# Gate and up matmuls as full-row matmuls with grouped remainders, or all as pairs of 64-row tiles

## The chip, the core and the metric

The kernel runs on one core of a Trainium2 chip. Its engines are named as in the profile: PE (TensorE: matmuls, and PEld its weight loads), DVE (VectorE), ACT (ScalarE), POOL (GpSimd) and SP (SyncE, which here only issues DMAs). The metric is the device time of one execution in microseconds (us). Times below are us unless another unit is given.

## The reference, cut to what matters

The sequence has 2048 rows, D = 576 columns, F = 4608 hidden columns; all tensors are bfloat16.

```python
kv = conv4(k, shift_k) * v                       # four taps along the rows
y = irfft(rfft(pad(kv)) * rfft(pad(ssm_k)))[:S]  # a long causal convolution
x = x + ga * (ln(x) * (1 + ca) + sa) * (y + kv * ssm_D)
h = ln(x) * (1 + cb) + sb
out = x + gb * ((silu(h @ w1) * (h @ w3)) @ w2)  # w1, w3: 576 x 4608, w2: 4608 x 576
```

ga, ca and the others are columns of silu(c) @ w_mod. The matmuls with w1 (the gate) and w3 (up) contract over 576 = 4 x 128 + 64 rows.

## The kernel before, in words

The 2048 rows go in four row blocks of 512 (each of two blocks of 256). For each row block `stream` computes h3 = silu(gate) * up, 36 items of 128 hidden columns by 512 rows, and `down` multiplies h3 with w2. Beside `stream` and `down` of row block r runs the convolution of the two blocks of row block r + 1, as a generator (`conv`, and `conv_second` for block 1) that `advance` steps forward: each step yields its cost, each item of `stream` adds to what is due. The convolution is done blockwise with Fourier matrices: `x_spectrum` and `w_spectrum` transform with matmuls (`forward` for blocks 0 and 1, `forward2` later), `pair` multiplies and adds spectra on DVE (operations of 128x3456), `inverse` transforms back with matmuls.

An item fills one PSUM tile `ps` of two banks, gate in the one and up in the other. The PSUM pool has four such tiles, which the items and the convolution's matmuls share. Of the five row tiles that are contracted, four have 128 rows and one has 64. `full` (line 916) does the eight matmuls with 128 rows; `rest` (line 927) does the two with 64 rows, gate from partitions 0 to 63 and up from 64 to 127, which PE runs side by side in the two halves of its array. Items are taken in groups of `size`, two, or four in the last row block, so that the remainders of the group stand together: early items full then rest, late items rest then full. `hide` then empties the tile with two ACT operations (sg, line 934, silu; u, line 936, a copy), DVE multiplies them into h3 (line 938), and `advance` lets the convolution go on.

A first pass, before row block 0's own stream, does rows 0 to 255 of the first 24 hidden chunks (six jobs of four chunks, where an item holds two chunks by 256 rows), while the convolution of block 1 is still under way. Row block 0 then does rows 256 to 511 of these chunks, in jobs of two items, alternating with jobs of four items that do whole chunks.

The weights come in jobs of four chunks (`load_w13`): four DMAs on SP, two of 512 KB (line 871) and two of 64 KB (line 872). There are two buffers `wst`; the last nine chunks of the tile h3 are a third one for the first six loads (FIRST_USE), when nothing of h3 stands there yet. The last three chunks of the first pass keep their weights for row block 0.

Layer norms: ACT sums rows and squares (`ln_sums`, tile junk, line 442, four operations for a block), POOL works out the scales in six small operations (`ln_scales`, lines 457 to 462), and ACT applies them (hg, line 502, and h2row, line 568). POOL's queue has little else.

Each engine takes its instructions in program order. SP's queue issues DMAs in order too, each after its own waits. PE's order is that in which the functions are called.

The lines that the change and the prediction's steps touch are these:

Of the kernel before, what the change touches and what calls it, by code (L numbers as in the profile page):

```python
# [27 lines left out]
FIRST_USE = (0, 1, 2, 0, 1, 2)  # L28
# [16 lines left out]
class _Kernel:  # L45
    def __init__(self, ctx, tc, q, k, v, shift_k, ssm_k, ssm_D, w1, w3, w2, c, w_mod, out):
        self.tc, self.nc = tc, tc.nc
        self.q, self.k, self.v = q, k, v
        self.shift_k, self.ssm_k, self.ssm_D = shift_k, ssm_k, ssm_D
        self.w1, self.w3, self.w2, self.c, self.w_mod, self.out = w1, w3, w2, c, w_mod, out  # L50
        pool = lambda name, **kw: ctx.enter_context(tc.tile_pool(name=name, **kw))
        self.const = pool("const", bufs=1)
        self.psum = pool("psum", bufs=4, space=bass.MemoryType.PSUM)
        self.dram = pool("spill", bufs=1, space=bass.MemoryType.DRAM)
        self.spec = pool("spec", bufs=4)
        self.wprev = pool("wprev", bufs=2)
        self.prod = pool("prod", bufs=1)
        self.acc = pool("acc", bufs=1)
        self.ld = pool("ld", bufs=1)
        self.kvp = pool("kvp", bufs=1)  # L60
        self.x1p = pool("x1p", bufs=4)
        self.lnp = pool("lnp", bufs=1)
        self.small = pool("small", bufs=4)
        self.hp = pool("hp", bufs=2)
        self.w2p = pool("w2p", bufs=NW2)
        self.xo, self.hg, self.accs, self.l1 = {}, {}, {}, {}
        self.X, self.V, self.Wl = {}, {}, {}
        self.n_w13, self.w13, self.kept = 0, {}, {}

# [4 lines left out]
    def setup(self):  # L74
        nc, const = self.nc, self.const
        nc.scalar.preload_act_table(ACT.Silu)
        self.ident = const.tile([P, P], BF16, name="ident")
        self.npi = const.tile([P, 1], F32, name="npi")
# [8 lines left out]
        self.wst.append(self.h3[:, NF - 9:NF, :])  # L87
# [205 lines left out]
    def forward(self, basis, rhs, dst):  # L293

        nc = self.nc
        for e in range(2):
            for cs in range(2):
                ps = self.ps()
                for cc in range(2):
                    for h in range(2):  # L300
                        nc.tensor.matmul(ps[:, h, 0:H], basis[:, cc * (e + 1), cs],
                                         rhs[:, cc, h * H:(h + 1) * H],
                                         start=(cc == 0), stop=(cc == 1))
                nc.scalar.copy(dst(e, cs).rearrange("p (h d) -> p h d", h=2), ps[:, :, 0:H])  # L304
                yield 0.4

    def forward2(self, basis, rhs, both, odd, diff):
# [3 lines left out]
        for cc, dst in ((0, both), (1, odd)):  # L311
            for cs in range(2):
                ps = self.ps()
                for h in range(2):
                    nc.tensor.matmul(ps[:, h, 0:H], basis[:, cc, cs], rhs[:, cc, h * H:(h + 1) * H],  # L315
                                     start=True, stop=True)
                nc.scalar.copy(dst[:, cs].rearrange("p (h d) -> p h d", h=2), ps[:, :, 0:H])  # L317
                yield -1.9
# [39 lines left out]
    def k_rows(self, s):  # L358
# [5 lines left out]
        for cc in range(2):  # L364
            for ct in range(5):
                nc.tensor.transpose(pt[:, cc, ct * P:(ct + 1) * P], nat[:, ct, cc:B:2],
                                    self.ident[:])
        nc.scalar.copy(kT[:], pt[:, :, 0:D])
# [162 lines left out]
    def inverse(self, s, cc):  # L531
        nc = self.nc
        z = self.accs[s]
        ps = self.ps()
# [4 lines left out]
        for i, (b, cs, row) in enumerate(terms):  # L539
            for h in range(2):  # L540
                nc.tensor.matmul(ps[:, h, 0:H], self.Fb[:, b, cs], z[:, row, h * H:(h + 1) * H],  # L541
                                 start=(i == 0), stop=(i == len(terms) - 1))
        return ps
# [27 lines left out]
    def turn(self, pt, cc):  # L571
        for ct in range(5):
            self.nc.tensor.transpose(pt[:, cc, ct * P:(ct + 1) * P],  # L573
                                     self.h2row[:, cc, ct * P:(ct + 1) * P], self.ident[:])
# [20 lines left out]
    def turned(self, s, pt, c0, n):  # L595
# [4 lines left out]
        for ct in range(5):  # L600
            dst = hT[:, ct, t * P:(t + n) * P].rearrange("p (c t) -> p c t", c=n)
            src = pt[:, c0:c0 + n, ct * P:(ct + 1) * P]
# [27 lines left out]
    def first_block(self):  # L630
# [62 lines left out]
        ps = [self.inverse(0, cc) for cc in range(2)]  # L693
# [39 lines left out]
    def outcome(self, s, fill, waits, between=None, quick=False):  # L733


        def steps():
# [4 lines left out]
            for cc in range(2):  # L741
                nc.scalar.copy(y[:, cc, :].rearrange("p (h d) -> p h d", h=2), self.inverse(s, cc)[:, :, 0:H])  # L742
# [118 lines left out]
    def load_w13(self, fc):  # L861
        nc = self.nc
        if self.n_w13 < len(FIRST_USE):
            t = self.wst[FIRST_USE[self.n_w13]]
        else:
            t = self.wst[self.n_w13 % NW13]
# [7 lines left out]
    def advance(self, cost):  # L874

        self.due += cost
        while self.due > 0 and self.steps is not None:
# [5 lines left out]
            self.spent += c  # L883

    def stream(self, r, jobs, rate, size):
# [11 lines left out]
        gus, ws = {}, {}  # L897
# [12 lines left out]
        def full(k, first):  # L910
            (fc, t0, t1, _, _), fi, m = items[k]
            w, n = ws[fc, t0, t1], t1 - t0
            for a in range(m):
                for i in range(2):
                    for ct in range(4):
                        nc.tensor.matmul(gus[k][:, i, a * n:(a + 1) * n],  # L916
                                         w[:, 5 * i + ct, (fi + a) * P:(fi + a + 1) * P], hT[:, ct, t0:t1],
                                         start=(first and ct == 0 and a == 0),
                                         stop=(not first and ct == 3 and a == m - 1))

        def rest(k, first):
            (fc, t0, t1, _, _), fi, m = items[k]
            w, n = ws[fc, t0, t1], t1 - t0
            for a in range(m):
                for i in range(2):
                    rows = slice(64 * i, 64 * i + 64)
                    nc.tensor.matmul(gus[k][:, i, a * n:(a + 1) * n],  # L927
                                     w[rows, 4, (fi + a) * P:(fi + a + 1) * P], hT[rows, 4, t0:t1],
                                     start=(first and a == 0), stop=(not first and a == m - 1))

        def hide(k):
# [9 lines left out]
            self.advance(rate * 2.05)  # L941
# [5 lines left out]
        for k in range(0, len(items), size):  # L947
            early, late = range(k, k + size // 2), range(k + size // 2, k + size)
            for m in early:
                begin(m)  # L950
                full(m, True)
            for m in early:
                rest(m, False)
            for m in late:
                begin(m)
                rest(m, True)
            for m in early:
                hide(m)
            for m in late:
                full(m, False)  # L960
                hide(m)
# [47 lines left out]
    def end(self):  # L1009
        self.advance(1e9)  # L1010

    def run(self):
# [5 lines left out]
        with self.tc.issue_after(last):  # L1018
            self.begin(self.conv_second())
            self.stream(0, [(fc, 0, 256, None, None) for fc in range(n1)], RATE1, 2)  # L1020
# [6 lines left out]
    def row_blocks(self, n1):  # L1027
        for r in range(NRB):
# [8 lines left out]
            if r == 0:  # L1037

                jobs = [(fc, 256, 512, self.kept[fc], None) for fc in (n1 - 3, n1 - 2, n1 - 1)]
# [3 lines left out]
                again = [(fc, 256, 512, None, None) for fc in range(n1 - 3)]  # L1043
# [5 lines left out]
            self.stream(r, jobs, rate, 4 if r == NRB - 1 else 2)  # L1049
# [55 lines left out]
```

## Time and profile before

| | us |
|---|---|
| median of three runs | 523.05 (522.37 to 525.87) |
| the profiled execution | 522.37 |
| its span | 520.6 |
| PE busy | 496.6 |
| DVE busy | 341.1 |
| ACT busy | 293.3 |
| POOL busy | 55.0 |
| idle of PE before gate/up matmuls of 128 rows, 128x512 | 3.5 |

| stage | stretch of the span | length |
|---|---|---|
| opening: block 0's convolution | 0 to 33.7 | 33.7 |
| first pass | 33.7 to 70 | 36.3 |
| row block 0: stream, down | 70 to 137, 137 to 172 | 67, 35 |
| row block 1: stream, down | 172 to 250, 250 to 293 | 78, 43 |
| row block 2: stream, down | 293 to 372.6, 372.6 to 409 | 79.6, 36.4 |
| row block 3: stream, down | 409 to 481, 481 to 520.6 | 72, 39.6 |

How to read the lines of a profile: a line of the order of time has its start, its length, the engine, the line of the kernel, the operation, output<-inputs with shapes, and how many equal ones are merged; in brackets the idle time before it and what ended it. The ends of matmuls are modelled and overlap the next one's start, so the distance of starts is what counts. In the table of the costliest groups a line has the busy time, the mean length in ns, and the engine's idle time before it by what ended it.

### The profile page before, as it was taken

What the parts mean: (1) busy time and instruction counts of PE and PEld (TensorE: products, weight loads), DVE (VectorE), ACT (ScalarE), POOL (GpSimd) and SP (SyncE); (2) the same over time, 40 slices, a digit from 0 to 9 for tenths busy, and PEclk for the clock granted to TensorE, in tenths of its full rate; (3) what the DMA queues carried; (4) which work ended last, traced back from release to release, by engine and by line L of the source; (5) the groups of instructions that cost most, each with busy time, mean ns of one, the idle gap of its engine ahead of it and who ended that gap; (6) DMA issues with size and microseconds to landing.
All of it is one profiled execution on the core that took longest, in us unless ns stands there. A gap on an engine that the chain in (4) does not pass through costs nothing.

```text
span 520.6 us, 8705 instructions
## 1 busy us (share of the span) xinstructions
PE 496.6 (95%) x3351; PEld 292.1 (56%) x3351; DVE 341.1 (66%) x515; ACT 293.3 (56%) x581; POOL 55.0 (11%) x109
## 2 busy tenths in 40 slices
PE   6988989999999999999997999999999999999996
PEld 3656766555687544344785643434588544444775
DVE  8799997999994355897999995389661212212012
ACT  5748679678543469759551465876816446446000
POOL 3403001304030001202001000120101000000000
PEclk9989999999999999999999999999999999999999
DMA  8996909566679953648999884454455553450462
GB/s 280 331 288 196 271 27 351 186 196 203 181 236 313 336 170 115 204 143 291 360 366 313 324 273 159 157 185 152 154 142 144 147 173 124 156 174 3 122 176 68
DMA packets 100989, 106.59 MB, mean 205 GB/s; under 512 B 5011, under 2 KB 93012, under 8 KB 100948
## 3 DMA queue, kind: packets, MB, share of 16 engines
q1 hardware_dynamic: 100926, 106.04, 63.8%
q8 instruction: 26, 0.43, 0.3%
q14 instruction: 15, 0.12, 0.1%
q10 hardware_dynamic: 22, 0.01, 0.0%
HBM read 94.82 MB, written 11.21 MB: 204 GB/s over the span
## 4 chain that ended last, share of the span: by engine, by line
PE 72%; DVE 13%; ACT 7%; DMA 5%; issue 2%; POOL 1%; SPq 0%; POOLq 0%; DVEq 0%; ACTq 0%
PE ps L916 38%; PE ps L979 23%; PE ps L927 6%; DMA w2t<-in_B_w_dram 3%; DVE p L412 2%; PE ps L315 2%; ACT junk L442 1%; DVE h L938 1%; DVE z L407 1%; DVE kv L337 1%; PE ps L541 1%; DVE z L414 1%; DMA wst<-in_B_w_dram 1%; DMA knat<-in_A_ssm_k_dram 1%; ACT X L304 1%
## 5 line engine op out<-in xcount | busy, mean ns | idle before, releaser
L916 PE MATMUL ps<-h2T,wst 128*128 128x512 bf16 (+1 forms) x1248 | 255.1, 356 | 3.5 <-ACT h2T L603 1.6
L916 PEld LDWEIGHTS <-wst 128*128 128x128 bf16 x1248 | 118.7, 98 | 124.0 <-issue 20.0
L934 ACT ACTIVATE sg<-ps 128x512 bf16<-128x512 f32 x144 | 87.0, 604 | 115.6 <-PE ps L927 69.7
L979 PE MATMUL ps<-w2t,h 128*128 128x288 bf16 x1152 | 145.8, 286 | 5.8 <-DMA w2t<-in_B_w_dram 3.9
L979 PEld LDWEIGHTS <-h 128*128 128x128 bf16 x1152 | 112.2, 98 | 35.6 <-issue 6.5
L938 DVE TENSOR_TENSOR h<-sg,u 128x512 bf16<-128x512 bf16 x144 | 60.4, 422 | 95.7 <-ACT u L936 95.7
L936 ACT CAST u<-ps 128x512 bf16<-128x512 f32 x144 | 84.8, 589 | 0.4 <-DVE h L938 0.4
L412 DVE TENSOR_TENSOR p<-X,V 128x3456 bf16<-128x3456 bf16 x28 | 54.7, 1952 | 7.6 <-DMA X<-Xd 6.0
L414 DVE TENSOR_TENSOR z<-z,p 128x3456 bf16<-128x3456 bf16 x28 | 54.7, 1952 | 0.2
L997 DVE TENSOR_TENSOR og<-ps,gbrow 128x288 bf16<-128x288 f32 x32 | 13.2, 450 | 48.8 <-PE ps L979 48.8
L927 PE MATMUL ps<-h2T,wst 64*128 64x512 bf16 (+1 forms) x312 | 40.8, 357 | 0.0
L442 ACT ACTIVATE junk<-x 128x576 bf16<-128x576 bf16 x54 | 37.7, 699 | 0.5
L603 ACT ACTIVATE h2T<-ps,sbcol,cbcol 128x256 bf16<-128x256 bf16 x35 | 16.7, 569 | 26.8 <-PE ps L573 26.8
L927 PEld LDWEIGHTS <-wst 64*128 64x128 bf16 x312 | 10.3, 94 | 26.6 <-issue 23.9
L457 POOL TENSOR_SCALAR l2m<-l2s 128x2 f32<-128x2 f32 x6 | 8.2, 1366 | 153.3 <-ACT junk L442 153.3
L336 DVE TENSOR_TENSOR kvt<-kh,shk 128x1152 bf16<-128x1152 bf16 x24 | 18.1, 753 | 6.7 <-DMA kh<-in_A_k_dram 6.6
L457 POOL TENSOR_SCALAR l1m<-l1s 128x2 f32<-128x2 f32 x7 | 5.9, 847 | 142.1 <-ACT junk L442 142.1
L568 ACT ACTIVATE h2row<-x,l2n,l2r 128x576 bf16<-128x576 bf16 (+1 forms) x24 | 13.8, 652 | 11.6 <-POOL l2n L462 11.6
L337 DVE TENSOR_TENSOR kv<-kv,kvt 128x1152 bf16<-128x1152 bf16 x24 | 18.1, 753 | 0.3
L317 ACT CAST X<-ps 128x576 bf16<-128x576 f32 x24 | 15.7, 664 | 0.0
L407 DVE TENSOR_TENSOR z<-X,V 128x3456 bf16<-128x3456 bf16 x7 | 13.7, 1952 | 1.8 <-DMA X<-Xd 1.8
L742 ACT CAST y<-ps 128x576 bf16<-128x576 f32 x14 | 8.4, 650 | 10.7 <-PE ps L541 10.6
(140 smaller groups left out, 377.5 us busy)
## 6 DMA issues: line engine op xcount, KB each, us to landing
wst<-in_B_w_dram SPq DMA_DIRECT2D x74, 512.0 KB, 4.6
w2t<-in_B_w_dram SPq DMA_DIRECT2D x72, 288.0 KB, 3.5
X<-Xd SPq DMA_DIRECT2D x8, 864.0 KB, 5.6
Xd<-X SPq DMA_DIRECT2D x6, 864.0 KB, 8.1
kh<-in_A_k_dram SPq DMA_DIRECT2D x7, 720.0 KB, 7.4
wst<-in_B_w_dram SPq DMA_DIRECT2D x74, 64.0 KB, 2.2
Vd<-V SPq DMA_DIRECT2D x4, 864.0 KB, 6.1
V<-Vd SPq DMA_DIRECT2D x4, 864.0 KB, 6.4
```

What stands on the lines that cost most here:

```text
L336: nc.vector.tensor_mul(tmp[:], kh[:, 3 - j:5 - j, :], tap(j))
L337: nc.vector.tensor_add(kv[:], kv[:], tmp[:])
L407: nc.vector.tensor_mul(self.accs[s][:], X[:], V[:])
L412: nc.vector.tensor_mul(p[:], X[:], V[:])
L414: nc.vector.tensor_add(z[:], z[:], p[:])
L442: self.nc.scalar.activation(junk[:], src[:, i, :], func, accum_out=out[:, col:col + 1])
L916: nc.tensor.matmul(gus[k][:, i, a * n:(a + 1) * n], w[:, 5 * i + ct, (fi + a) * P:(fi + a + 1) * P], hT[:, ct, t0:t1], start=(first and ct ...
L927: nc.tensor.matmul(gus[k][:, i, a * n:(a + 1) * n], w[rows, 4, (fi + a) * P:(fi + a + 1) * P], hT[rows, 4, t0:t1], start=(first and a == 0 ...
L934: nc.scalar.activation(sg[:], gus[k][:, 0, :], ACT.Silu)
L936: nc.scalar.copy(u[:], gus[k][:, 1, :])
L938: nc.vector.tensor_mul(self.h3[:, f:f + m, t0:t1], sg[:].rearrange("p (a t) -> p a t", a=m), u[:].rearrange("p (a t) -> p a t", a=m))
L979: nc.tensor.matmul(acc[t], self.h3[:, f0 + f, t * P:(t + 1) * P], w[:, f, :], start=(f0 + f == 0), stop=(f0 + f == NF - 1))
```

## The change

All gate and up matmuls, and the convolution's matmuls and transposes that are called while a stream is running (`self.halves`), are done with 64 rows: what was one matmul over 128 rows is two over 64, one for each half of the partitions. At any time one half of the array works on gate and the other on up (for the convolution: on the left and on the right 288 columns), so the two write different banks of the tile; then they swap. Between the two parts each bank passes from one half of the array to the other. For that a token is used: a memset of one element on POOL waits for the last matmul of the first part, and the first matmul of the second part waits for the memset. The items are staggered: the first part of item k+1 is issued before the second part of item k, and for the convolution `advance` breaks off after a first part, so that a part of the stream stands between. An item's first part has ten half matmuls (five pairs), its second eight. The buffer in h3 is no longer used: `wst` has two buffers, the first pass keeps two jobs' weights for row block 0 in place of three, and one job more is read again. Groups of two or four items are gone.

```diff
+    def token(self):
+        first = self.newest()
+        self.nc.gpsimd.memset(self.tok[:], 0.0)
+        self.wait_for(self.newest(), first)
+        return self.newest()
+
+    def two_banks(self, outs, terms):
+        mm = self.nc.tensor.matmul
+        if not self.halves:
+            for n, term in enumerate(terms):
+                for i in range(2):
+                    mm(outs[i], *term(i, slice(0, P)), start=(n == 0), stop=(n == len(terms) - 1))
+            return
+        for swap in range(2):
+            for n, term in enumerate(terms):
+                for rows, i in ((slice(0, 64), swap), (slice(64, P), 1 - swap)):
+                    mm(outs[i], *term(i, rows), start=(swap == 0 and n == 0),
+                       stop=(swap == 1 and n == len(terms) - 1))
+                    if swap == 1 and n == 0 and i == 1:
+                        self.wait_for(self.newest(), mark)
+            if swap == 0:
+                mark = self.token()
+                self.pause = True
+                yield 0.0
...
-        self.wst.append(self.h3[:, NF - 9:NF, :])
...
     def advance(self, cost):
...
             self.spent += c
+            if self.pause:
+                self.pause = False
+                break
...
-        def full(k, first):
+        def part(k, swap):
             (fc, t0, t1, _, _), fi, m = items[k]
             w, n = ws[fc, t0, t1], t1 - t0
             for a in range(m):
-                for i in range(2):
-                    for ct in range(4):
+                cols = slice((fi + a) * P, (fi + a + 1) * P)
+                for ct in range(4 if swap else 5):
+                    for rows, i in ((slice(0, 64), swap), (slice(64, P), 1 - swap)):
                         nc.tensor.matmul(gus[k][:, i, a * n:(a + 1) * n],
-                                         w[:, 5 * i + ct, (fi + a) * P:(fi + a + 1) * P], hT[:, ct, t0:t1],
-                                         start=(first and ct == 0 and a == 0),
-                                         stop=(not first and ct == 3 and a == m - 1))
+                                         w[rows, 5 * i + ct if ct < 4 else 4, cols], hT[rows, ct, t0:t1],
+                                         start=swap == 0 and ct == 0 and a == 0,
+                                         stop=swap == 1 and ct == 3 and a == m - 1)
+                        if swap == 1 and ct == 0 and a == 0 and i == 1:
+                            self.wait_for(self.newest(), marks[k])
+            if swap == 0:
+                marks[k] = self.token()
...
-        for k in range(0, len(items), size):
-            early, late = range(k, k + size // 2), range(k + size // 2, k + size)
-            for m in early:
-                begin(m)
-                full(m, True)
-            for m in early:
-                rest(m, False)
-            for m in late:
-                begin(m)
-                rest(m, True)
-            for m in early:
-                hide(m)
-            for m in late:
-                full(m, False)
-                hide(m)
+        self.halves = True
+        for k in range(len(items) + 1):
+            if k < len(items):
+                begin(k)
+                part(k, 0)
+                self.advance(rate * 2.05 * 5 / 9)
+            if k > 0:
+                part(k - 1, 1)
+                hide(k - 1)
+                self.advance(rate * 2.05 * 4 / 9)
+        self.halves = False
...
-                jobs = [(fc, 256, 512, self.kept[fc], None) for fc in (n1 - 3, n1 - 2, n1 - 1)]
+                jobs = [(fc, 256, 512, self.kept[fc], None) for fc in (n1 - 2, n1 - 1)]
...
-                again = [(fc, 256, 512, None, None) for fc in range(n1 - 3)]
+                again = [(fc, 256, 512, None, None) for fc in range(n1 - 2)]
```

In the changed program PE has 4881 matmuls in place of 3351, and POOL 196 tokens, 144 for the items and 52 for the convolution. Where a stream is running, a block's ten transposes of 128x128 become 18 or 20 of 64x64, and the copy of kT is two ACT operations.

## The prediction

> **What bounds the kernel now.** I read the page's busy line first, then a table by stage, then the instructions in order of time inside one stage, then the waits and the DMA issues.
>
> ```profile
> PE 496.6 (95%) x3351; PEld 292.1 (56%) x3351; DVE 341.1 (66%) x515; ACT 293.3 (56%) x581; POOL 55.0 (11%) x109
> PEclk9989999999999999999999999999999999999999
> ```
>
> TensorE (PE) is busy nearly throughout, at the full granted clock. The table by stage (columns: stretch, length, PE, weight loads, DVE, ACT, POOL, clock, DMA share, GB/s) shows the first pass (24 half chunks), then the gate/up streams of row blocks 0, 1, 2 and 3; the down projections lie between them.
>
> ```profile
> 33.70:70.00 36.30, 34.33 (x310) 26.31 (x310) 33.24 (x55) 24.31 (x47) 5.59 (x8) 0.96 0.69 202
> 70.00:137.00 67.00, 61.65 (x457) 38.02 (x455) 62.96 (x82) 51.25 (x104) 12.29 (x18) 1.00 0.65 213
> 172.00:250.00 78.00, 78.00 (x403) 32.32 (x401) 54.74 (x82) 57.51 (x116) 7.75 (x18) 1.00 0.63 210
> 293.00:372.60 79.60, 79.19 (x411) 33.12 (x409) 58.49 (x83) 55.35 (x111) 5.16 (x14) 1.00 0.55 179
> 409.00:481.00 72.00, 72.00 (x363) 30.34 (x362) 16.47 (x41) 36.74 (x71) 0.00 (x0) 1.00 0.40 130
> ```
>
> DVE is nearly full in the first two rows (33.2 of 36.3, 63.0 of 67.0), where PE has little slack too; in the last three PE alone sets the time. What the change attacks is visible in PE's order of time in row block 1:
>
> ```profile
> 202.35 1.89 PE L916 MATMUL ps<-h2T,wst 128*128 128x512 bf16 x8
> 204.18 0.61 PE L927 MATMUL ps<-h2T,wst 64*128 64x512 bf16 x4
> 204.71 0.42 PE L315 MATMUL ps<-kv,Fb 128*128 128x288 bf16 x2
> ```
>
> In the last stage 16 full matmuls follow each other in 3.45 us, 0.216 each. Here eight take 204.18-202.35 = 1.83, 0.10 more than 8 x 0.216; the two pairs of half-row matmuls take 0.53, again 0.10 more than 2 x 0.216. So a pair costs one full matmul, and each change between full rows and half rows costs 0.10. Weight loads also show it: idle 0.42 before each change.
>
> Three more views carry the costs: ACT's bursts beside PE, Pool's chain, and the weight loads.
>
> ```profile
> 238.50 1.63 ACT L502 ACTIVATE hg<-x,l1n,l1r 128x576 bf16<-128x576 bf16 x2
> 239.41 0.60 PE L927 MATMUL ps<-h2T,wst 64*128 64x512 bf16 x4
> ...
> 240.20 3.62 PE L916 MATMUL ps<-h2T,wst 128*128 128x512 bf16 x16
> ...
> 241.89 0.59 ACT L934 ACTIVATE sg<-ps 128x512 bf16<-128x512 f32 x1
> 243.03 0.59 ACT L936 CAST u<-ps 128x512 bf16<-128x512 f32 x1
> 243.50 0.70 ACT L442 ACTIVATE junk<-x 128x576 bf16<-128x576 bf16 x1
> 244.28 3.63 PE L916 MATMUL ps<-h2T,wst 128*128 128x512 bf16 x16
> ```
>
> ACT works without a gap from 238.0 to 247 here, hg, layer-norm sums (junk), X, sg and u in turn, and PE runs on: four PSUM tiles were enough.
>
> ```profile
> 0.24 0.10 POOL L1089 MEMSET const-float32-0.0<- 128x1 f32 x1 [0.24 <-issue]
> 199.20 0.19 POOL L458 TENSOR_SCALAR l1v<-l1q 128x2 f32<-128x2 f32 x1
> 200.54 0.20 POOL L462 TENSOR_TENSOR l1n<-l1m,l1r 128x2 f32<-128x2 f32 x1
> ```
> ```profile
> wst<-in_B_w_dram SPq DMA_DIRECT2D x74, 512.0 KB, 4.6
> ```
>
> A memset takes 0.10; a layer norm's chain on Pool takes 1.5 from l1v to l1n, and the waits put 299 us of Pool's idle time down to ACT's sums. A 512 KB weight transfer lands 4.6 after its issue.
>
> **The change part by part.** *Switches removed.* The 144 gate/up items stand now in 54 groups of two and 9 of four, each with two switches: 126 x 0.10 = 12.6 us, by stage 1.2, 2.4, 3.6, 3.6, 1.8. Afterwards nine pairs an item (18 half matmuls) take the nine slots of today. Left are about eight switches at the down projections and gate piece: +0.8. The convolution's matmuls are 288 wide; 512- and 256-wide pairs both cost what full ones cost (0.216, 0.109), so theirs cost nothing extra. The transposes become up to 20 of 64x64; bounds are half and equal the 0.66 that ten take today, which is small either way.
>
> *Tokens.* An item's first part (5 pairs, 1.08) is followed by the other item's second part (4 pairs, 0.86) and the next item's first part before its own second part: 1.9 us for PE's end (0.17 after the last start), the memset (0.10, up to 0.20 for other tiny operations) and two semaphores. Hidden. A convolution token has one stream part, 0.86 or more: hidden also, against about 0.5. What ends the cover is Pool's queue: a token issued behind a layer-norm chain waits for ACT's sums and then 1.5 us. Row block 1's first chain, by the changed order: two drains of 0.47 and four sums of 0.77 after PE's part, chain 1.5, token: 6.0; PE arrives at 5.0. It waits 1.0.
>
> *PSUM tiles held longer.* An item is now open for two first and two second parts, 3.9 us, where an early item is open for 2.3; a convolution tile is open for a stream part more. Two items, the convolution's tile and the one being drained fill all four, and in the order the next item's first matmul waits for the copy of the convolution tile just finished. PE's cover for it is 0.86+0.12, the copy needs 0.17+0.66+0.05: 0.1 us left. So each burst on ACT in a convolution phase now stalls PE: the two hg operations (1.6) cost 1.1; the sums of the second l1, worked through in order, 2.2; hg and the l2 sums together 3.7 (sg 3.8 after the convolution's first matmul, u's end 5.6, PE ready at 2.2). In the profile such stalls are nil (PE idles 0.4 in all of row block 1). Row block 1: 1.0+1.1+2.2+3.7 = 8.0 less 3.6, +4.4. Row block 2 has the same bursts, the last one at the end of its stream (2.2): 6.6-3.6 = +3.0. Bounds each: -3.6, if a burst on ACT stays free as above, and +8. I take the worked orders, since the rows for ACT are these very operations.
>
> The Trainium skill's page "TensorEngine Tiling (Array Packing)", in Restrictions and Gotchas, speaks against the change here: it warns that row tiling increases PSUM pressure, different row tiles needing different banks. Today's rows show none of it, with 0.4 of idle; by today's row these two stages would gain 7.2, by the page they would lose part or all of it.
>
> *Weight buffers.* In the staggered order a chunk's buffer is free only after the next job's first part. Today's reload has the whole next job as cover. Both 512 KB transfers are now issued together at the end: 0.2+4.6+0.5 for the second = 5.3 us. With four-item jobs the cover is three items, 5.8: just hidden. In row block 0 two-item jobs alternate with four-item ones and leave one item, 1.95 (with convolution matmuls 2.45 and 3.0). Four loads wait: 2.85+3.35+2.3+3.35 = 11.9. Queued behind the waiting matmul are the stream and the convolution's matmuls, so ACT and DVE starve with them. Bursts on ACT there cost about 5 more; 2.4 of switches go; of today's 6.8 us of PE stalls some 4 go, as DVE gets ahead. +10.5. Bounds: -2.4, if DVE covers all, and +16. On SP the waiting loads also stand ahead of k, x and Xd transfers, which are early enough. One more chunk is read (1.18 MB), beside a DMA that is 0.65 busy: nothing.
>
> *First pass.* The third buffer goes, so four loads have one-item covers; the first wait falls beside PE's wait for kv, which ended at 45.4. The x spectrum's sixteen matmuls, 2.1 in one piece at 45.4, are now spread over two items, +3.9, and DVE's sums wait for them at 48.4 on the chain that ended last. Less 1.2: +2.7; bounds -1.2 and +6.
>
> *Row block 3* has no convolution: -1.8; at worst 0.3 a load, +0.6. The down projections keep full rows: 0.
>
> Sum: 2.7+10.5+4.4+3.0-1.8+0.8 = +19.6 on the profiled execution's 522.4 (span 520.6 and 1.8 around it) is 542.0. Runs of before have the median 523.05, 0.7 above it; within the error I forecast 542.
>
> **The rivals.** *Only the buffers cost.* PSUM and ACT behave as in the profile, so row blocks 1 and 2 keep -3.6 each, and row block 0 pays 11.9-2.4-4 = +5.5. 2.7+5.5-3.6-3.6-1.8+0.8 = 0: 522. For it speaks that nine us of ACT without a gap were free; against it that all four tiles are now held.
>
> *Faster.* PE's switches are the bound everywhere and every wait lies beneath work that DVE or PE has anyway: -12.6+0.8 = -11.8, 511. For it: PE's 95%. Its place is row block 0, where DVE's 63 of 67 would have to cover the loads; it decides while all waits together stay below 11.8, against some 31 by the sums above.
>
> *Pool is slower than assumed.* Operations on Pool took up to 0.68 in place of 0.20 beside a DVE operation, and the longest, beside five of them, 3.2. If a memset is held like that, by one DVE operation of 1.95, the 52 convolution tokens lose about 0.6 each: +31, some 570. Against it: the memset rows of 0.10. The Trainium skill's page "SBUF — State Buffer", Who interferes with whom, says that two-input Vector operations hold up only Pool operations that read SBUF; by it the memsets go free, by the row they don't, and no memset in the trace lies beside such an operation.
>
> **How the numbers follow.** Forecast 0.58, buffers only 0.16, faster 0.14, Pool slower 0.12. Changes of 1%, 5 us, are about what a measurement of this kernel can tell from none. Faster holds the 0.14. Within 1%: 0.14, most of the second case and a little of the first. Slower: 0.72, the rest. The range leaves out the faster case and the upper part of the Pool case: 521 to 565. The forecast's own range is 528 to 558, by the bounds of row block 0 (-2.4 to +16) and the two next (each up to 4 either way), which will not all fall on one side.
>
> **What would show it.** Right: no idle between half-row matmuls of different lines, nine pairs in 1.94; PE waits for wst by DMA, near 3 us, four times in row block 0; PE waits for ACT (X, u) in row blocks 1 and 2, and for Pool's token behind l1n and l2n; row block 3 near 70. Wrong: row blocks 1 and 2 at 74 to 76 (then PSUM was not short); row block 0 at 67 or below (then DVE covered the loads); token memsets lasting over 0.5, or waits for them away from the layer norms (then Pool is the cost).

## The result and the profile after

The changed kernel takes 601.3 us (median of four runs, 600.6 to 602.8) beside 522.7 for the kernel before on the same chip: a ratio of 1.150, 95% interval 1.144 to 1.156. The profiled execution took 601.6, its span is 599.5. I had forecast 542 with a range of 521 to 565: slower was right, the size was not.

TensorE's busy line and its granted clock, in 40 slices, of the kernel after:

```profile
PE 513.7 (86%) x4881; PEld 325.0 (54%) x4881; DVE 345.9 (58%) x515; ACT 298.1 (50%) x586; POOL 65.6 (11%) x305
PEclk9887878898889999999979999998899999999999
```

Busy time grew by 17 us only; the rest of the 79 is time in which TensorE did nothing. And the clock line, nines with a single eight before, has sevens and eights nearly all through the first pass and row block 0 and a few more in row blocks 1 and 2, the stages in which a convolution runs beside the matmuls. The table by stage of the kernel after (stretch, length, PE, weight loads, DVE, ACT, POOL, clock, DMA share, GB/s):

```profile
32.70:70.00 37.30, 25.14 (x340) 19.62 (x340) 20.59 (x28) 17.17 (x34) 9.44 (x19) 0.82 0.47 147
70.00:178.50 108.50, 79.58 (x971) 53.91 (x968) 81.21 (x112) 57.09 (x114) 12.83 (x67) 0.87 0.47 152
218.00:313.30 95.30, 80.51 (x730) 42.31 (x730) 59.01 (x84) 58.96 (x116) 13.05 (x68) 0.95 0.53 179
357.90:452.00 94.10, 79.89 (x731) 40.60 (x730) 56.42 (x80) 57.33 (x114) 9.95 (x68) 0.96 0.45 143
489.80:560.00 70.20, 69.93 (x649) 31.35 (x648) 15.99 (x40) 36.99 (x70) 3.21 (x36) 1.00 0.42 134
```

The first two rows are the first pass and row block 0 (together 96.3 us before, from the start of the first to the start of the last stream matmul; 145.9 now), then row blocks 1, 2 and 3 (78.0 to 95.2, 78.1 to 94.1, 71.6 to 70.2). Only the last one, which has no convolution, gained. In the stages where DVE was nearly full it now works 21 us of 37 and 81 of 108, so the amount of its work isn't the bound.

What TensorE waited for, in all stages (us in total, times, longest):

```profile
PE ps L974 <- DMA wst<-in_B_w_dram: 19.0, 10, 3.2
PE ps L974 <- POOL tok L83: 12.8, 4, 7.1
PE ps L98 <- POOL tok L83: 12.2, 9, 4.0
PE ps L98 <- ACT u L988: 11.0, 7, 3.3
PE ps L974 <- ACT u L988: 10.2, 13, 2.7
...
PE ps L974 <- ACT X L352: 3.4, 3, 1.6
```

Three sorts of waits, each of 19 to 25 us: weights (19.0), tokens (25.0), PSUM tiles that ScalarE had not read yet (24.6). In the kernel before no such line, for a stream's or the convolution's matmuls, is above 1. The fourth part of the loss is no wait. Three stretches of the table by stage inside row block 1:

```profile
278.20:281.10 2.90, 0.25 (x4) 0.00 (x0) 2.90 (x3) 1.03 (x2) 0.00 (x0) 1.00 0.60 209
281.20:282.20 1.00, 1.00 (x10) 0.56 (x11) 1.00 (x3) 0.00 (x0) 0.00 (x0) 1.00 0.00 0
282.30:285.60 3.30, 3.30 (x20) 1.44 (x18) 1.33 (x4) 3.01 (x6) 0.09 (x1) 0.52 0.00 0
```

TensorE waits for most of 2.9 us, runs ten half matmuls in 1.0, and then for 3.3 us has a granted clock of 0.52, where 20 half matmuls are started in place of some 31. PE shows as busy all through these 3.3 us: only the clock column tells. In the trace the half clock comes in stretches of 3.41 us or a multiple; there are 61.4 us of it in the span, 3.4 before.

Count each matmul at the distance of starts that its width has at full clock, a pair of halves as one full matmul, and put down the same time nearly once more to the clock where it starts at half clock. The four gate/up stages then divide so: the matmuls themselves 299.2 (300.1 before), lost to half clock 24.5 (1.4), switches between full and half rows 0.2 (12.4), waits and small gaps, which is the rest, 81.4 (10.1). That is -0.9+23.1-12.2+71.3 = +81.3, as the stage lengths give; the opening and the down projections are 0.8 and 1.5 shorter. The switches went as forecast. The waits and the clock ate more than seven times as much.

### The profile page after: what moved, and what is told of

It is laid out like the page before. It is cut to its first block, busy times and chain, and to the rows that moved or that the text cites. A ratio compares the mean times of both kernels' runs of the same rounds, so it can differ in the third digit from the quotient of the medians.

```text
span 599.5 us, 12152 instructions
## 1 busy us (share of the span) xinstructions
PE 513.7 (86%) x4881; PEld 325.0 (54%) x4881; DVE 345.9 (58%) x515; ACT 298.1 (50%) x586; POOL 65.6 (11%) x305
## 4 chain that ended last, share of the span: by engine, by line
PE 54%; DMA 13%; DVE 13%; ACT 11%; POOL 4%; issue 3%; SPq 1%; ACTq 0%; POOLq 0%
PE ps L974 29%; PE ps L1026 20%; DMA wst<-in_B_w_dram 7%; DMA w2t<-in_B_w_dram 4%; ACT junk L488 4%; DVE z L460 4%; DVE p L458 3%; ACT u L988 2%; ACT sg L986 2%; DMA h<-in_w_mod_dram 2%; POOL l1m L503 2%; PE ps L98 1%; PE ps L93 1%; ACT hg L548 1%; DVE h L990 1%
## 5 line engine op out<-in xcount | busy, mean ns | idle before, releaser
L974 PE MATMUL ps<-h2T,wst 64*128 64x512 bf16 (+1 forms) x3024 | 324.7, 364 | 46.9 <-DMA wst<-in_B_w_dram 19.0
L974 PEld LDWEIGHTS <-wst 64*128 64x128 bf16 x3024 | 170.4, 99 | 178.3 <-issue 30.3
L83 POOL MEMSET tok<- 1x1 f32 x196 | 17.5, 89 | 366.0 <-PE ps L974 305.6
L98 PE MATMUL ps<-kv,Fb 64*128 64x288 bf16 x128 | 18.8, 306 | 14.4 <-POOL tok L83 7.9
L98 PEld LDWEIGHTS <-Fb 64*128 64x128 bf16 x208 | 14.2, 105 | 30.3 <-issue 13.3
L799 ACT CAST y<-ps 128x576 bf16<-128x576 f32 x14 | 8.8, 647 | 18.4 <-PE ps L93 12.7
L98 PE MATMUL ps<-kT,Fk 64*128 64x288 bf16 x64 | 10.1, 296 | 5.7 <-POOL tok L83 4.3
```

What stands on the lines that cost most here:

```text
L83: self.nc.gpsimd.memset(self.tok[:], 0.0)
L98: mm(outs[i], *term(i, rows), start=(swap == 0 and n == 0), stop=(swap == 1 and n == len(terms) - 1))
L974: nc.tensor.matmul(gus[k][:, i, a * n:(a + 1) * n], w[rows, 5 * i + ct if ct < 4 else 4, cols], hT[rows, ct, t0:t1], start=swap == 0 and c ...
```

## The experiments

**Theory.** Three separate sorts of wait, not one bound, and on top of each the half clock that follows a long idle time of TensorE. **Rivals:** one bound behind all waits (VectorE), so that taking one away only uncovers the next; the halved convolution as such; the weight buffers as such.

**Tokens behind a layer norm.** The longest wait, in the first pass of the kernel after (timeline):

```profile
35.68 6.40 POOL L503 TENSOR_SCALAR l1m<-l1s 128x2 f32<-128x2 f32 x1 [1.11 <-ACT junk L488]
...
44.29 0.23 POOL L83 MEMSET tok<- 1x1 f32 x2
44.43 3.81 PE L974 MATMUL ps<-h2T,wst 64*128 64x256 bf16 x34 [7.07 <-POOL tok L83]
```

The two tokens take 0.23 together. Ahead of them on Pool is a chain of six operations on 128x2 numbers, of which the first took 6.40 us; the sums that it needs had been there at its start. Of TensorE's token waits in the trace, eight, with 24.0 us, stand behind such a chain or its first operation. This one lasted 8.7 us from its first operation to its last; the other seven lasted 2.4 to 4.2, and Pool could start them only after 1.8 to 3.6 us of waiting for ScalarE's sums. The first edit issues the chains later:

```
 def gate_stats(self, s):
...
-        self.l1[s] = self.ln_scales(ssum, ssq, "l1")
+        self.l1[s] = ssum, ssq
+    def gate_scales(self, s):
+        with self.behind(self.nc.gpsimd):
+            self.l1[s] = self.ln_scales(*self.l1[s], "l1")
```

gate_scales is called after kv_rows or, for the second block of two, after the next pair; the l2 chains are moved likewise, by 4.0 of planned work.

> The staggered kernel (601.3 us, profiled span 599.5) with one thing moved: Pool's layer-norm chains are issued after tokens that come later, once ScalarE's sums are due, instead of ahead of them. Theory (three kinds of waits, each followed by a lower clock): TensorE waited 25.1 us for tokens in four stages (7.1, 7.3, 3.2, 7.5), nearly all behind a chain; about 20 of them go, and of the 63 us at half clock some 15 with them, worth 8: 573, between 565 and 583. Rival (the tokens only cover VectorE and ScalarE being late): other waits take their place, 590 to 601. The 7.1 in the first pass may stay in part, since one Pool operation there took 6.4 beside VectorE.

607.1 us (604.1 to 609.7), ratio to before 1.162 (1.154 to 1.169): no gain, 6 us worse. The first pass with row block 0 became 9 shorter, row blocks 1 and 2 longer by 8 and 5; waits for tokens rose from 25.0 to 33.0, and one token was waited for 14.0 us. Timeline of this kernel:

```profile
255.17 12.36 POOL L503 TENSOR_SCALAR l1m<-l1s 128x2 f32<-128x2 f32 x1
...
265.50 1.95 DVE L460 TENSOR_TENSOR z<-z,p 128x3456 bf16<-128x3456 bf16 x1
...
272.85 1.46 PE L988 MATMUL ps<-h2T,wst 64*128 64x512 bf16 x6 [13.99 <-POOL tok L83]
```

The theory's cause was wrong in one point. It isn't only the sums that hold a chain (here they were long done): an operation that takes 0.22 elsewhere lasts 12.36, beside a row of fourteen DVE operations without a gap, and ends at 267.5, when the row has its first gap, of 0.035. Pool's queue is in order, so the token stands behind it, and TensorE behind the token. So the chains went to VectorE, the tokens staying on Pool:

```
-        e = self.nc.gpsimd
+        e = self.nc.vector if n == 2 else self.nc.gpsimd
...
-        e.tensor_tensor(rstd[:], var[:], self.neghalf[:, 0:n], op=ALU.pow)
+        if n == 2:
+            e.tensor_scalar(rstd[:], var[:], -0.5, 1.5, op0=ALU.mult, op1=ALU.add)
+        else: ...
```

> The staggered kernel with the layer-norm chains issued late, as in the run before, and on VectorE instead of Pool, so that from the first weight chunks on Pool has tokens and two small roots alone; the reciprocal root of the 13 chains is replaced by the first step of its Newton iteration. In the run with late chains on Pool (607) one scale operation of 128x2 took 12.4 us and one 8.8 beside VectorE operations without a gap, and a token behind them was waited for 14.0. Theory (Pool's queue holds the token because its small operations are held by VectorE): no token is waited for above 1 us, token waits fall from 25.1 to below 5, half clock from 63 to about 45: 575, between 565 and 585. Rival (moving them only shows that VectorE is late; it now does 78 small operations more): 595 or more.

587.7 us (586.2 to 589.9), ratio 1.126 (1.121 to 1.131), 13.6 less than the changed kernel. TensorE's waits for tokens in this run are one line:

```profile
PE ps L98 <- POOL tok L83: 1.0, 5, 0.3
```

25.0 became 1.0, so it is shown that the chains on Pool's queue held the tokens. The run moves the chains late as well, which alone gained nothing, and replaces the root by the first step of its Newton iteration. The time fell by half of what the theory said, since waits for u rose from 21.2 to 26.0 and for weights from 19.0 to 22.1. Half clock went from 61.4 to 51.2 us.

**Products that VectorE makes late.** In the stretch at 278 above TensorE waits for u. Timeline of the kernel after:

```profile
275.70 1.95 DVE L460 TENSOR_TENSOR z<-z,p 128x3456 bf16<-128x3456 bf16 x1
...
277.68 1.96 DVE L458 TENSOR_TENSOR p<-X,V 128x3456 bf16<-128x3456 bf16 x1
...
279.56 0.42 DVE L990 TENSOR_TENSOR h<-sg,u 128x512 bf16<-128x512 bf16 x1
...
280.07 0.60 ACT L986 ACTIVATE sg<-ps 128x512 bf16<-128x512 f32 x1 [3.79 <-DVE h L990]
...
281.20 4.88 PE L974 MATMUL ps<-h2T,wst 64*128 64x512 bf16 x28 [2.75 <-ACT u L988]
```

ScalarE had nothing to do for 3.79. Its two buffers for sg and u were full, because the product h stood behind two convolution operations of 1.95 each. The edit gives u four buffers in the memory of sg:

```
-            sg = self.hp.tile([P, RB], BF16, name="sg", tag="sg")
-            nc.scalar.activation(sg[:], gus[k][:, 0, :], ACT.Silu)
+            h = self.h3[:, f:f + m, t0:t1]
+            nc.scalar.activation(h, gus[k][:, 0, :].rearrange(...), ACT.Silu)
...
-            nc.vector.tensor_mul(self.h3[:, f:f + m, t0:t1], sg[:]..., u[:]...)
+            nc.vector.tensor_mul(h, h, u[:]...)
```

> The staggered kernel with the silu written straight into h3 and multiplied there in place, so that the memory of sg gives u four buffers in place of two; nothing else. Theory: TensorE's waits for u (21.1 us, up to 3.3 each) come from ScalarE waiting for VectorE's product h (37.6), which stands behind convolution products of 1.95 and holds both buffers; with four buffers ScalarE's waits fall below 10, some 15 of TensorE's go and 4 of clock: 582, between 573 and 590. Rival (the prediction's reason: bursts on ScalarE hold the PSUM tiles): 596 or more, the waits for u as before.

591.2 us (587.9 to 594.4), ratio 1.132 (1.123 to 1.142), 10 less, between the theory's range and the rival. ScalarE's waits for h, first in the kernel after, then in this one:

```profile
ACT sg L986 <- DVE h L990: 37.6, 18, 3.8
```

```profile
ACT u L989 <- DVE h L990: 7.7, 4, 3.1
```

TensorE's waits for u fell from 21.2 to 11.7. So a little under half of them went with the deeper buffers and were VectorE's lateness; the prediction had put them all down to ScalarE's bursts.

**Weights.** In one run the third buffer is given back, as in the kernel before (FIRST_USE, the tail of h3, three kept chunks). In another all loads of the first pass and row block 0 after the first two chunks are left out.

```
-        t = self.wst[self.n_w13 % NW13]
+        t = self.wst[FIRST_USE[self.n_w13]] if self.n_w13 < len(FIRST_USE) else self.wst[self.n_w13 % NW13]
```

> The staggered kernel with the third weight buffer (the tail of h3) and the third kept chunk back, so one chunk less is read again. Theory: of the 20.3 us of waits for weights the first pass's (4.4, and about 4 just after it) go, with perhaps 6 us of half clock, worth 3: 590, between 584 and 597. Rival (the buffers are the main loss): 575 or less. Rival (VectorE or tokens are just as late there): 599 to 602.

595.3 us (594.4 to 595.8), ratio 1.139 (1.133 to 1.145): 6 less, though waits for weights fell from 19.0 to 5.3.

```
+        if 2 < self.n_w13 <= 13:
+            return
```

> The staggered kernel without the weight loads of the first pass and of row block 0 after the first two chunks (stale weights are used there): prices all 20.3 us of waits for weights. By their sum and 8 us of half clock after them it would be 573. By the third buffer's run, where 13.7 us of these waits went and only 6 came off, it is 588 to 592: VectorE's or the tokens' waits fill the place. I expect 588; 575 or less would mean that the buffers alone carry a third of the loss.

591.8 us (590.2 to 592.5), ratio 1.133 (1.128 to 1.139). With waits for weights down to 1.4, those for tokens and u are 26.4 and 23.7 and the down projections begin to wait for u (5.4). Taking away all 19 us gains 9.4.

**The convolution in full rows.** Only gate and up stay in staggered pairs (self.halves stays False).

```
-        self.halves = True
         for k in range(len(items) + 1):
```

> The staggered kernel with the convolution back in full rows: no tokens, pauses or half rows there, the gate/up pairs and their tokens as they are. It has 143 switches between full and half rows in place of 43: +10. Theory of the waits: the convolution's own token waits (12.3) go and its PSUM tile is held shorter (some 5 of the 21 that TensorE waited for u), but gate/up tokens behind Pool's chains and weight loads stay: 585 to 600. Rival (the halved convolution is the loss): 540 or less.

597.1 us (596.3 to 598.4), ratio 1.143 (1.137 to 1.149). With 100 switches back, some 10 us, the halved convolution would cost about 14 otherwise; that is an estimate, since waits for weights rose from 19.0 to 30.6 in this run. It is not the main loss. That rival is out.

**All three remedies.**

> Chains late and on VectorE (root by its first Newton step), four buffers for u, and the third weight buffer, all on the staggered kernel. Singly the last two gave -10 and -6. Theory (separate waits, each with its share of lower clock): the gains add to some -42 to -50 and half clock falls below 30 us: 555, between 545 and 567; what stays are waits for X, for VectorE's late products and the four one-item loads. Rival (all waits cover one bound, VectorE's work in row block 0): 575 to 590.

562.8 us (559.3 to 564.3), ratio 1.077 (1.072 to 1.083): 38.5 off, where the single gains are 13.6+10.0+6.0 = 29.6. The waits do cover one another in part, and taking away all of them gives more than the sum of each. So the rival of one bound is out. The theory's 42 to 50 was too much by a few, and half clock, which it put below 30 us, is still 39.3.

**ScalarE's bursts.** What stayed were 18.4 us of waits for u and 4.8 for X. The prediction had named bursts on ScalarE, and the kernel after has one where it had said (timeline):

```profile
294.90 1.63 ACT L548 ACTIVATE hg<-x,l1n,l1r 128x576 bf16<-128x576 bf16 x2
...
299.19 0.67 ACT L488 ACTIVATE junk<-x 128x576 bf16<-128x576 bf16 x1
...
299.86 0.57 ACT L988 CAST u<-ps 128x512 bf16<-128x512 f32 x1
300.32 0.65 ACT L352 CAST X<-ps 128x576 bf16<-128x576 f32 x1
300.48 0.42 PE L98 MATMUL ps<-kv,Fb 64*128 64x288 bf16 x2 [3.31 <-ACT u L988]
```

ScalarE works with no gap above 0.03 from 294.90 (hg, then four sums, junk, with sg and u between them), and the convolution's next matmul waits 3.31 for a tile. The sums were taken out of the kernel with the three remedies, at first with constants written by Pool in their place:

```
+        if ssum.shape[-1] == 2:
+            for out in (ssum, ssq):
+                self.nc.gpsimd.memset(out[:, col:col + 1], 576.0)
+            return
```

> The kernel with the three remedies (562.8) and without ScalarE's sums for the layer norms (constants written by Pool in their place): takes the longest bursts off ScalarE, four sums of 0.77 together. TensorE still waited 18.4 us for u there and 4.8 for X. Theory (these bursts hold the PSUM tiles, the part of the prediction that was sized 8.0 and 6.6 in row blocks 1 and 2): 10 of it and 4 of half clock go: 549, between 544 and 554. Rival (VectorE's late products hold them): 558 or more.

563.5 us (560.9 to 564.7), ratio 1.079 (1.073 to 1.084). Not what the theory said, but not a test of it either: waits for u fell to 8.7, and 11.1 us of token waits came in their place, since Pool's constants stood ahead of tokens as the chains had. So again, with one constant for all:

```
+        if n == 2:
+            ssum = ssq = self.fixed
```

> The kernel with the three remedies (562.8) and without ScalarE's sums for the layer norms: the scales are worked out from a constant that is written once, so nothing stands on Pool in their place. Theory (ScalarE's bursts hold the PSUM tiles): waits for u and X fall from 23.2 to about 12 as in the run before, tokens stay below 3: 551, between 545 and 556. Rival (VectorE is as late and its waits come out instead): 559 to 563.

554.6 us (553.9 to 557.2), ratio 1.065 (1.060 to 1.069): 8.2 less, waits for u 11.0 and for X 3.3, tokens 3.6. So the sums were behind some 9 of the 23.2 us of PSUM waits that were left; what holds the tiles in the other 14.3 no run here separates.

**The clock by itself.** In the kernel before, in its last row block, TensorE is made to wait eight times, for ten small memsets on Pool, or in a second kernel for five:

```
+        def pause():
+            first = self.newest()
+            for _ in range(10):
+                nc.gpsimd.memset(self.h2T[0][:, 0, 0:256], 0.0)
+                self.wait_for(self.newest(), first)
+            marks.append(self.newest())
```

> The clock alone, in the kernel before: in its last row block (71.7 us, no convolution, full clock) TensorE waits after each of eight groups of four items for ten small memsets on Pool, about 3 us. If half clock follows idling (theory), most of the eight pauses are followed by a stretch of 3.4 us at half clock, worth 1.7 each: the stage grows by 8 x 3.3 of waiting and 8 to 14 of clock: 106 to 112, the kernel 557 to 564. If it has another cause (rival), the stage grows by the waits alone: 98, and the clock stays 1.00.

> The same with five memsets, pauses of about 1.7 us. In the staggered kernel waits of 1.6 and 1.8 us were mostly not followed by half clock and those of 2.8 to 4.1 mostly were. Theory: the stage grows by 8 x 1.8 of waiting and no clock: 86, the kernel 537. Rival (any wait lowers the clock): 93 or more.

567.6 us (565.2 to 570.1), ratio 1.087 (1.079 to 1.095), and 540.1 (538.5 to 541.7), ratio 1.034 (1.027 to 1.042). The row of that stage, with the long and with the short pauses:

```profile
411.60:528.50 116.90, 86.52 (x362) 32.84 (x360) 16.52 (x42) 36.74 (x70) 24.88 (x80) 0.88 0.25 81
```

```profile
409.50:500.10 90.60, 74.93 (x362) 29.97 (x360) 16.54 (x42) 36.80 (x70) 12.47 (x40) 0.98 0.32 104
```

The matmuls are the same 71.8 us (71.6 and the last one's 0.2). Both stages came out above the forecasts of 106 to 112 and 86, since the pauses were longer than planned. A long pause parts two starts by 4.18 (3.96 more than usual): 8 x 3.96 = 31.7, and the clock of 0.88 means eight stretches of 3.41 at half, 8 x 1.7 = 13.6; 71.8+31.7+13.6 = 117.1, measured 116.9. Every one of the eight was followed by such a stretch. The short pauses part them by 2.12 more: 8 x 2.12 = 17.0, one stretch of half clock 1.7, together 90.5, measured 90.6. The end of one of the eight long pauses; the matmuls after it start 0.427 apart (timeline of the kernel with long pauses):

```profile
437.05 5.26 PE L926 MATMUL ps<-h2T,wst 128*128 128x512 bf16 x16 [3.80 <-POOL h2T L961]
```

So idling lowers the clock. The Trainium skill's page "TensorE: Matmul & The Clock Gate" (HAM oscillation) warns of gaps of TensorE above about 3.4 us; here waits of 2.75 and 2.81 were followed by half clock as well, and one of 3.2 at 127 was not.

The length of a wait alone does not decide, and the traces show what does. In each of the 18 traces of this case all stretches of half clock start on one fixed raster of 3.41 us. Take the raster's slots at full clock from 33 us on, and in each the time in which TensorE stood idle, worked out from the distances of its matmuls' starts. Of 2450 slots with less than 1.9 us of it none was followed by a slot at half clock, of 44 with 1.9 to 2.2 us 12 were, and of 110 with more than 2.2 us all were. The long pauses idled TensorE for 3.96 and happened to fill a slot nearly whole each time, 3.36 us of it or more. Of the short ones, 2.1 each, six were split by the raster, with at most 1.84 in one slot, and of the two that lay within one slot one was followed. The wait of 3.2 at 127 was split into 1.4 and 2.0; the one at 278 had 2.2 in one slot. Eight of eight and one of eight are thus no rates for waits of these lengths: they depend on where on the raster the pauses fell.

In the changed kernel I also put 14 dummy matmuls where three jobs of row block 0 waited for weights, so that TensorE worked there.

```
+            if r == 0 and items[k][0][0:2] in ((6, 0), (7, 0), (3, 256)) and items[k][1] == 0:
+                for _ in range(14):
+                    nc.tensor.matmul(gus[k][:, 0, :], self.ident[:], hT[:, 0, :], start=True, stop=True)
```

> The staggered kernel with 14 dummy matmuls of 512 columns (3.0 us) put ahead of the first part of three jobs in row block 0, into the PSUM tile that the job then overwrites: TensorE works where it waited 3.1 to 3.3 us for weights (starts 110.9, 130.8, 172.0). The waits stay about as long, so only the clock can gain. Theory (half clock comes after TensorE has idled): the stretches of 3.4 us at half clock after the first and third of them go, 2 x 1.7 less 0.6 for six switches: -3, 598. Rival (the clock has another cause, or the time at half clock is hidden by other engines): 601 to 603.

602.6 us (600.0 to 605.1), ratio 1.154 (1.149 to 1.159). The two half-clock stretches after those waits are gone, and the first pass with row block 0 is 140.6 in place of 145.9; but the opening, the down projections after row block 0 and row block 2 are 1.9, 2.8 and 2.6 longer, and the total is the same. It shows neither a gain nor its absence.

**Tiles without pairs.** Groups of four items in the kernel before, in row blocks 1 and 2 too, fill all four PSUM tiles with no half-row pairs or tokens added.

```
-            self.stream(r, jobs, rate, 4 if r == NRB - 1 else 2)
+            self.stream(r, jobs, rate, 4 if r > 0 else 2)
```

> The kernel before with groups of four items instead of two in row blocks 1 and 2 as well: 36 switches fewer there, no half-row pairs in the convolution, no tokens. Four items open fill all four PSUM tiles, so a convolution step has to wait for a drained one. By the switches alone (rival): -3.6 or a little less, 518. Theory (open tiles without slack turn ScalarE's and VectorE's lateness into waits of TensorE): each of 18 groups loses some 0.7 and half clock follows a few of the longer ones: +8 to +20, 536.

529.8 us (527.7 to 534.3), ratio 1.018 (1.012 to 1.025): slower with 36 switches fewer. In this run the convolution's matmuls wait for tiles that were free before:

```profile
PE ps L315 <- ACT u L936: 5.2, 10, 0.9
```

So open tiles without slack cost time by themselves, though less than I had put: the waits are short, and after the opening half clock follows once. Not all of the 6.8 us is theirs: the transposes wait 3.3 for h2row, which they do not in the kernel before.

**What the kernel before can use.** Staggered pairs in the last row block alone, four buffers for u alone, and both. A size of 1 stands for the changed kernel's part and token.

```
-            self.stream(r, jobs, rate, 4 if r == NRB - 1 else 2)
+            self.stream(r, jobs, rate, 1 if r == NRB - 1 else 2)
```

> The kernel before with only its last row block's gate/up in staggered half-row pairs with tokens: no convolution beside it, 16 switches fewer. That stage went from 71.7 to 70.2 in the changed kernel: 521.5 - 1.5 = 520.0, a ratio of 0.997. Rival (the stage gains only since the block before it ended differently): 0.999 to 1.001.

> The kernel before with the silu written into h3 and four buffers for u. ScalarE waited 12.1 us for VectorE's product there, and TensorE's own stalls were 10 us, all in the first pass and row block 0. Theory: two open items leave a group's slack, so little of that reaches TensorE: 520, between 517 and 522. Rival (it gives what it gave in the changed kernel, 10 us): 512.

> The kernel before with both: staggered half-row pairs in the last row block alone, and the silu written into h3 with four buffers for u. If the two single results add: 0.9973, some 521.0 with the interval just touching 1. If they are noise: 0.999 to 1.001. Theory says that row block 3 gives 0.7 to 1.5 us and the buffers 1 or less in row block 0, so 0.996 to 0.999.

522.0 us, ratio 0.999 (0.997 to 1.002); 521.3, ratio 0.998 (0.995 to 1.001); both together 521.4, ratio 0.998 (0.995 to 1.001). With the pairs alone the stage is 70.8 in place of 71.6. None can be told from the kernel before, and no staggered version beat it.

## Why the prediction was wrong

- **Switches and pairs: right.** A pair costs one full matmul (216 ns from pair to pair, also when its halves run 55 ns out of step), the 12 us of switches are gone, row block 3 gained 1.5 against 1.8, the down projections changed by -1.5 in sum.
- **Tokens: wrong, and with the clock the largest of the misses.** The step that failed is "Hidden" with "It waits 1.0", 25.0 measured. It had the right place, a token issued behind a layer-norm chain that waits for ScalarE's sums, but priced one of the eight chains that TensorE came to wait for, and took 1.5 us for it, the last four operations of a chain that ran undisturbed. The chain that it priced cost 2.2, its six operations lasting 3.6; the other 22.8 us lie where it had put nothing. The rival "Pool is slower" asked whether the memsets are held beside VectorE; they are not (0.089 each), but operations of the chain ahead of them are, one for 6.40. The evidence had been on the page of before, whose Pool operations took "up to 0.68" and 3.2.
- **The clock: left out.** No step said what a wait costs beyond its own length. 24.5 us were lost to half clock in the four stages. The before profile, at full clock otherwise, shows it only in one stretch of 3.41 us, at 33.3. That gaps bring it is what the page cited above says; it should have stood beside each term of 2 us or more.
- **PSUM tiles: right in place and nearly in size, wrong in part of the cause.** Row blocks 1 and 2 were to lose 7.0 and 6.6 to ScalarE (8.0 less the token's 1.0); TensorE's waits for u and X were 10.0 and 6.6. But in the whole kernel nearly half of the waits for u were VectorE's late product holding ScalarE's two buffers, which no step mentions; that row block 2 came out at its 6.6 exactly is luck.
- **Weight buffers: right, a little small.** 11.9 in row block 0 against 14.5, and 4.4 in the first pass, which I had costed at 3.9 for all its waits; it waited another 7.1 for a token. What I had not seen is how little of it stands alone: without any of these waits the kernel is 9.4 faster, not 19.
- **The sum.** My stalls come to 35.4 us (3.9, 11.9+5, 8.0, 6.6), the measured ones named above to 68.6, and to 70.9 with 2.3 for kT and h2T; so 24 of tokens and 11.5 of the others were missing, 35.5, and 24.5 of clock: 542+35.5+24.5 = 602, beside 601.6 profiled. So close an agreement is partly luck, since the smaller terms of the prediction's sum were not measured one by one.

The waits that I had called hidden were each hidden by TensorE's own work on an open item, and so only as long as no other wait had used that up: with four tiles open, two weight buffers and one in-order queue for the tokens, there was one cover for three things.

## What to carry to other kernels

When a change makes one engine wait on another's in-order queue, price the slowest operation that can stand ahead in that queue, beside whatever runs at that time, not the operation waited for. Give every TensorE wait of some 2.2 us or more up to 1.7 us more for the clock (24.5 us beside 81 of waits and gaps here), and read the clock row before trusting a busy share. Where an engine is busy 95% of the time, 12 us of visible waste can be worth less than the slack (tiles, buffers, order) that its removal uses up.

## What the runs showed of the hardware

- Half clock comes in stretches of 3.41 us or multiples of it, on one raster in each trace, and follows a raster slot in which TensorE stood idle for more than 2.2 us (110 of 110 slots), not one with less than 1.9 (0 of 2450), from 33 us on; in the openings of 12 of the 18 traces a stretch that starts at 25.5 to 28.2 us follows no such slot, and no run here tells why. Matmuls of 512 columns start 0.427 apart in it, in place of 0.216.
- A Pool operation on 128x2 numbers took 0.22 alone and 6.40, 8.80 and 12.36 beside two-input DVE operations that followed each other without a gap; token memsets took 0.09, at most 0.10. In the kernel before, the one after and six of the runs all eleven such Pool operations above 2.5 us ended 0.07 to 0.09 after DVE's row came to its first gap, of 0.034 or 0.035. The Trainium skill's page "SBUF — State Buffer" (Who interferes with whom) says that two-input Vector operations contend only with Pool operations that read SBUF, which agrees; that one may be held over fourteen such operations in a row, and not just one, is what I had not expected.
- Two 64-row tiles need not run in step: pairs whose halves start 55 ns apart follow each other every 216 ns as well.
